# Decayed attention and two MoE layers on one core: where the attention stage does its side work

## The chip, the cores and the metric

The kernel runs on one core of a Trainium2 chip. The metric is device time in microseconds, from one execution of the whole program. The kernel before takes 567.04 us (median of three runs, 565.8 to 567.11).

## The reference

The input of the first MoE layer is the output of a linear attention with decay: 2 batches, 8 heads, 768 tokens, heads 64 wide. Per head there is one decay `lam`, and the reference goes over the tokens in blocks:

```python
for b in range(nb):
    intra = einsum('bhic,bhjc->bhij', qb, kb) * Dmask      # lam ** (i - j) for i >= j
    intra = einsum('bhij,bhjd->bhid', intra, vb)
    inter = einsum('bhid,bhde->bhie', qb * lam_pow, kv_state)
    out[:, :, sl] = intra + inter
    kv_state = lam_block * kv_state + einsum('bhsd,bhse->bhde', kb * rev_pow, vb)
```

Two MoE layers follow on 1536 tokens (512 features, 2048 hidden): `h = x @ w_in; g = h * clip(h + 3, 0, 6) / 6; y = g @ w_out`, and then `h = relu(y @ w_in2); out = (h * h) @ w_out2`.

## The kernel before

**Attention.** The 1536 tokens are cut into 12 chunks of 128 (`NC`), even chunks from batch 0, odd ones from batch 1; each batch has its own running state. A chunk goes through these steps, in the program's names:

- `load_chunk` (line 258): four transfers of 256 KB, kT, q, k and v, on the SP queue (only q of chunk 0 on ScalarE's queue). Five chunk buffers rotate.
- `scores` (350): TensorE multiplies keys and queries, 16 matmuls (L357), into a pair of PSUM banks; VectorE multiplies them by the decay mask into A (L368, two instructions).
- `prepare` (326): GpSimd multiplies the queries by the decay powers `lpow`, giving qs (L330); ScalarE multiplies the keys by their decay to the chunk's end, giving kd, in eight instructions of 128x64, one for each head (L342).
- `old_state` (378): TensorE multiplies qs by the state of two chunks ago, the same batch's last one (L389), into a bank px, of which there are two (`px_room`).
- `new_state` (396): TensorE multiplies kd and v (L407). ScalarE scales the old state by the chunk's decay into kvs, four instructions of 128x64 (L421), and VectorE adds the two in one instruction of 128x256 (L426; for the first chunk of a batch it only copies, L414).
- `values` (430): TensorE multiplies A and v into px (L440). ScalarE copies px to xf (L451, the first eight chunks only) and rounds it to xh (L453); VectorE writes the residual xl = px - xh (L456). With that the bank px is free again.

The decay masks and powers are made at the start by scans on VectorE (L308, L318). `warming` (295) runs matmuls of a zeroed tile that nothing reads.

**MoE.** TensorE multiplies in pairs of rounded and residual parts: `hidden` (L669), `quad` (L700, on sums of weights and of tokens in place of eight products) and `project` (L755). Weights come packed and are decoded by `decode` (501): two ScalarE instructions (L516, L520), three on VectorE (L525, L531, L535), the rounded part on ScalarE (L538), and a sum and the residual on VectorE (L539, L542). Three buffers for `w_in` tiles are there during the attention; the others open when its last chunk is through (`lend`, 481). `token_sums` (583) forms four sums and differences of 128x1024 of the tokens for the quads, once per layer, on VectorE (L596), and splits them (L616, L612, L614). `weight_sums` (551) does the same for weights on GpSimd (L563, L576).

**The order of the work.** The program first collects all operations in a list (`plan.op`), each with an engine, a cost from `COST`, what it needs and which buffers it takes and gives back. `Plan.run` (94) then lays them out in time: TensorE keeps the order of the list, and on the other engines the operation that can start first is taken next, by its due time where several can. GpSimd and those VectorE operations whose cost name begins with d are kept apart in time (`port`). The kernel issues instructions in the order that comes out, so costs and list order set the order of every queue. The chip then runs each queue in order, with waits on semaphores.

Of the kernel before, what the change touches and what calls it, by code (L numbers as in the profile page):

```python
# [9 lines left out]
F32 = mybir.dt.float32  # L10
# [4 lines left out]
AF = mybir.ActivationFunctionType  # L15
ALU = mybir.AluOpType
PSUM = bass.MemoryType.PSUM

P = 128
BLOCKS = 3  # L20
GROUP = 4
WARM = (8, 6)

COST = {
    "psc": 1.10, "inter": 1.02, "pst": 0.61, "av": 0.88, "unit": 2.72, "high": 1.81, "low": 0.91, "part": 1.36,
    "v512": (0.60, 0.69), "v256": (0.335, 0.42),
    "d512": (0.60, 0.69), "d512s": (0.36, 0.44), "d256": (0.335, 0.42), "d1024": (1.13, 1.21), "dsums": (1.35, 1.44),
    "s64x4": (0.50, 0.60), "s64x8": (1.00, 1.10),
    "s512": (0.53, 0.63), "s512r": (0.57, 0.67), "s512b": (0.59, 0.69), "s512p": (0.48, 0.59), "s1024": (0.96, 1.06),
    "p512": (1.30, 1.40), "p512b": (1.06, 1.16), "p256": (0.70, 0.80), "p1024": (2.40, 2.50), "psums": (3.30, 3.40),  # L30
    "load": (1.30, 3.60), "chunk": (0.66, 2.30),
# [24 lines left out]
class Plan:  # L56
# [111 lines left out]
def decay_attention_moe_moe(  # L168
# [47 lines left out]
    plan = Plan()  # L216
    op = plan.op

    def tile_of(shape, dt, tag, name=None):
        return sb.tile(shape, dt, tag=tag, name=name or tag)  # L220
# [12 lines left out]
        (py_room if slot < 3 else ph_room).free.append((slot, t))  # L233


    idle = tile_of([P, 512], F32, "lpow", "idle")
    nc.vector.memset(idle, 0.0)
    lams = tile_of([P, H + NP], F32, "lams")
    lam_h, lam_p = lams[:, :H], lams[:, H:]
# [15 lines left out]
    part = lambda c, n: chunk_t[chunk_hold[c].slot][:, ("kT", "k", "v", "q").index(n), :]  # L255
    loaded = {}

    def load_chunk(c):
        hold = chunk_hold[c]
        for n, src in (("kT", kT), ("q", qT), ("k", k), ("v", v)):  # L260

            def do(n=n, src=src):
                (nc.scalar if c == 0 and n == "q" else nc.sync).dma_start(out=part(c, n), in_=src[chunk_of[c]])

            loaded[c, n] = op("SP", "chunk", do, take=[hold], due=2.6 * c - 10)


    A_t = [tile_of([P, NP, 2, P], F32, f"A{i}") for i in range(2)]
    qs_t = tile_of([P, 2, NP, P], F32, "qs")
    kd_t = tile_of([P, 2, H, D], F32, "kd")  # L270
    lpow_t, kvs_t = {}, {}
    A_room, qs_room, kd_room = Room(0, 1), Room(0, 1), Room(0, 1)

    xh = [tile_of([P, KD, N], F32R, f"xh{j}") for j in range(BLOCKS)]
# [17 lines left out]
    s7_t = []  # L292


    def warming(widths):
        x = idle.bitcast(BF16)
        for n in widths:
            nc.tensor.matmul(banks[0][:, :n], x[:, :P], x[:, :n], start=True, stop=True)  # L298

    px_of, sums_in, s_hold = {}, {}, {}  # L300
    scans = []

    def attention():
        A_op, av_op, kv_op, qs_op, kd_op, int_op, kvs_op = {}, {}, {}, {}, {}, {}, {}
        A_hold, qs_hold, kd_hold, px_hold = {}, {}, {}, {}

        def scan_decay(h):
# [7 lines left out]
        def scan_power(a):  # L315
            if not a:
                lpow_t[0] = tile_of([P, NP, P], F32, "lpow")
            nc.vector.tensor_tensor_scan(  # L318
                lpow_t[0][:, a, :], lam_p[:, a : a + 1].to_broadcast([P, P]), zero.to_broadcast([P, P]), 1.0,
                op0=ALU.mult, op1=ALU.add,  # L320
            )

        for c in range(NC):
            load_chunk(c)

        def prepare(c):
            if c > 1:

                def do():
                    nc.gpsimd.tensor_tensor(  # L330
                        qs_t[:, qs_hold[c].slot].rearrange("p a i -> p (a i)"), part(c, "q"),
                        lpow_t[0].rearrange("p a i -> p (a i)"), op=ALU.mult,
                    )

                qs_hold[c] = Hold(qs_room)
                chunk_hold[c].left += 1
                qs_op[c] = op("POOL", "p512", do, [loaded[c, "q"], *scans], take=[qs_hold[c]], give=[chunk_hold[c]])
            if c < NC - 2:

                def do():  # L340
                    for h in range(H):
                        nc.scalar.activation(  # L342
                            kd_t[:, kd_hold[c].slot, h, :], part(c, "k")[:, h * D : (h + 1) * D], AF.Copy,
                            scale=decay[:, h // 2, h % 2, P - 1 : P],
                        )

                kd_hold[c] = Hold(kd_room)
                kd_op[c] = op("ACT", "s64x8", do, [loaded[c, "k"], *decays], take=[kd_hold[c]])

        def scores(c):  # L350

            def do():
                ps = [b.rearrange("p (a i) -> p a i", i=P) for b in pairs[hold.slot]]
                for a in range(NP):
                    i = slice(a * P, (a + 1) * P)
                    for t, r in enumerate(halves):
                        nc.tensor.matmul(  # L357
                            ps[t][:, a, :], part(c, "kT")[r, i], part(c, "q")[r, i], start=True, stop=True
                        )

            hold = Hold(pair_room, 2)
            hold.pass_on = pass_pair if c >= NC - 2 else None
            o = op("PE", "psc", do, [loaded[c, "kT"], loaded[c, "q"]], take=[hold])
            if not c:
                op("PE", 1.3, lambda: warming([512] * WARM[1]), [o])

            def mask(t):
                nc.vector.tensor_tensor(  # L368
                    A_t[A_hold[c].slot][:, :, t, :], pairs[hold.slot][t].rearrange("p (a i) -> p a i", i=P),
                    decay[:, :, t, :], op=ALU.mult,  # L370
                )

            A_hold[c] = Hold(A_room)
            A_op[c] = [
                op("DVE", "v512", lambda t=t: mask(t), [o, *decays], take=[A_hold[c]], give=[hold]) for t in range(2)
            ]
# [19 lines left out]
        def new_state(c):  # L396
            if c >= NC - 2:
                return
            first = c < 2
            kv_old, kv_new = kv[c % 2][(c // 2 + 1) % 2], kv[c % 2][c // 2 % 2]  # L400
            hold = Hold(pst_room)
            hold.pass_on = pass_bank if NC - 4 <= c else None
            ps = lambda: banks[hold.slot][:, : NP * D].rearrange("p (a d) -> p a d", d=D)

            def do():
                for h in range(H):
                    nc.tensor.matmul(  # L407
                        ps()[halves[h % 2], h // 2, :], kd_t[:, kd_hold[c].slot, h, :], part(c, "v")[:, h * D : (h + 1) * D],
                        start=True, stop=True,
                    )  # L410

            pst = op("PE", "pst", do, [kd_op[c], loaded[c, "v"]], take=[hold], give=[kd_hold[c]])
            if first:
                kv_op[c] = op("DVE", "v256", lambda: nc.vector.tensor_copy(kv_new, ps()), [pst], give=[hold])  # L414
            else:
                s = Hold(ts_room)

                def scale():
                    kvs_t[c] = tile_of([P, KD, HALF], F32, "Ts", f"kvs{c}")[:, :, :D]
                    for a in range(NP):  # L420
                        nc.scalar.activation(kvs_t[c][:, a, :], kv_old[:, a, :], AF.Copy, scale=lpow_t[0][:, a, P - 1 : P])  # L421

                kvs_op[c] = op("ACT", "s64x4", scale, [kv_op[c - 2], *scans], take=[s])
                readers = [int_op.get(c - 2), kvs_op.get(c - 2)]
                kv_op[c] = op(
                    "DVE", "v256", lambda: nc.vector.tensor_tensor(kv_new, ps(), kvs_t.pop(c), op=ALU.add),  # L426
                    [pst, kvs_op[c], *readers], give=[hold, s],
                )

        def values(c):  # L430
# [27 lines left out]
            )  # L458
            x_ops[0, j] += [hi, lo]

        prepare(0)
        scores(0)
        for a in range(NP):
            scans.append(op("DVE", "v256", lambda a=a: scan_power(a)))
        prepare(1)
        new_state(0)
        old_state(0)
        values(0)
        scores(1)
        for c in range(1, NC):  # L470
            if c + 1 < NC:
                scores(c + 1)
                prepare(c + 1)
            old_state(c)
            new_state(c)
            values(c)
        return av_op

    lent = {}
# [103 lines left out]
    def token_sums(layer, old):  # L583
# [8 lines left out]
        def add(n, tag, a, b, sign, needs, take, give=()):  # L592

            def do():
                stage[n] = tile_of([P, KH, N], F32, tag, f"s{n}")
                nc.vector.tensor_tensor(stage[n], a(), b(), op=sign)  # L596

            return op("DVE", "d1024", do, needs, take=take, give=give)

        def split(n, o, give, wait=()):  # L600

# [201 lines left out]
    nc.gpsimd.memset(zero, 0.0)  # L803
    nc.gpsimd.memset(three, 3.0)
    warming([512] * WARM[0])
    plan.clock.update(PE=4.3, DVE=3.0, ACT=1.5, POOL=3.5, SP=1.0)
    attention()


# [126 lines left out]
```

## Time and profile before

| | |
|---|---|
| median of three runs | 567.04 us |
| the profiled execution | 565.54 us |
| its span, first to last instruction | 563.7 us |
| TensorE busy | 554.6 us, 98% |
| VectorE busy | 398.7 us, 71% |
| ScalarE busy | 348.4 us, 62% |
| GpSimd busy | 89.2 us, 16% |
| mean granted TensorE clock | 0.996 |

All times of the trace count from the start of the span. In the rows, PE is TensorE and PEld its weight loads, DVE is VectorE, ACT is ScalarE, POOL is GpSimd and SP is the sync engine, from which most transfers start; L342 is line 342 of the kernel. The granted clock is a share of 2.4 GHz: 1.00 is that level, 0.50 is 1.2 GHz. Busy shares are averages over the two stages, which differ much, so the rows below are taken stage by stage.

### The profile page before, as it was taken

What the parts mean: (1) busy time and instruction counts of PE and PEld (TensorE: products, weight loads), DVE (VectorE), ACT (ScalarE), POOL (GpSimd) and SP (SyncE); (2) the same over time, 40 slices, a digit from 0 to 9 for tenths busy, and PEclk for the clock granted to TensorE, in tenths of its full rate; (3) what the DMA queues carried; (4) which work ended last, traced back from release to release, by engine and by line L of the source; (5) the groups of instructions that cost most, each with busy time, mean ns of one, the idle gap of its engine ahead of it and who ended that gap; (6) DMA issues with size and microseconds to landing.
All of it is one profiled execution on the core that took longest, in us unless ns stands there. A gap on an engine that the chain in (4) does not pass through costs nothing.

```text
span 563.7 us, 7855 instructions
## 1 busy us (share of the span) xinstructions
PE 554.6 (98%) x2950; PEld 458.0 (81%) x2950; DVE 398.7 (71%) x647; ACT 348.4 (62%) x657; POOL 89.2 (16%) x78
## 2 busy tenths in 40 slices
PE   8988999999999999999999999999999999999997
PEld 6877888888888888888888888888888888888885
DVE  6759999858894698659999885138792589446222
ACT  6996885658552676148655996368752896168120
POOL 2230004330312103210000003210320121210000
PEclk9998999999999999999999999999999999999999
DMA  8982323302230032202330331102230033000112
GB/s 315 407 326 77 112 76 112 112 1 76 74 130 21 11 122 93 74 0 76 106 119 0 100 124 39 37 1 82 98 120 1 25 126 112 1 0 1 74 58 93
DMA packets 18038, 49.80 MB, mean 88 GB/s; under 512 B 2128, under 2 KB 2128, under 8 KB 18000
## 3 DMA queue, kind: packets, MB, share of 16 engines
q1 hardware_dynamic: 17856, 49.04, 24.9%
q8 instruction: 23, 0.38, 0.3%
q10 hardware_dynamic: 144, 0.26, 0.1%
q14 instruction: 15, 0.12, 0.1%
HBM read 46.14 MB, written 3.15 MB: 87 GB/s over the span
## 4 chain that ended last, share of the span: by engine, by line
PE 94%; ACT 5%; DVE 0%; issue 0%
PE b L755 46%; PE b L669 23%; PE b L700 20%; ACT kd L342 2%; PE b L357 1%; PE b L440 1%; PE b L389 1%; PE b L298 1%; ACT kvs L421 1%; PE b L407 1%; ACT xh L453 1%; ACT xf L451 0%; ACT da L516 0%; ACT dt L520 0%; DVE xl L456 0%
## 5 line engine op out<-in xcount | busy, mean ns | idle before, releaser
L779 DVE TENSOR_TENSOR acc<-acc,b 128x512 f32<-128x512 f32 x72 | 49.3, 686 | 62.1 <-PE b L755 61.9
L669 PE MATMUL b<-xh,wi 128*128 128x512 f32 x240 | 76.6, 389 | 0.0
L755 PE MATMUL b<-gC,wo 128*128 128x512 f32 x228 | 70.0, 389 | 0.0
L755 PE MATMUL b<-wo,gC 128*128 128x512 f32 x228 | 68.7, 389 | 0.0
L563 POOL TENSOR_TENSOR Tsum<-dt,dt 128x256 f32<-128x256 f32 x12 | 15.7, 1308 | 276.2 <-DVE dt L539 142.6
L669 PEld LDWEIGHTS b<-xh,wi 128*128 128x128 f32 x240 | 45.1, 188 | 9.5 <-issue 0.2
L650 ACT ACTIVATE gs<-b 128x512 f32<-128x512 f32 x48 | 28.1, 590 | 37.7 <-PE b L669 15.0
L535 DVE SCALAR_TENSOR_TENSOR da<-raw,da 128x512 int32<-128x512 int32 x64 | 50.3, 797 | 0.9
L644 ACT ACTIVATE gs<-b,three 128x512 f32<-128x512 f32 x48 | 32.6, 685 | 29.0 <-PE b L700 16.5
L755 PEld LDWEIGHTS b<-gC,wo 128*128 128x128 f32 x228 | 42.8, 188 | 8.9
L755 PEld LDWEIGHTS b<-wo,gC 128*128 128x128 f32 x228 | 42.8, 188 | 8.9
L516 ACT ACTIVATE da<-raw 128x512 f32<-128x512 f32 x64 | 42.1, 670 | 7.6 <-DVE dt L539 7.1
L669 PE MATMUL b<-xl,wi 128*128 128x512 f32 x120 | 46.7, 389 | 0.0
L576 POOL TENSOR_TENSOR Tl<-Tsum,Th 128x1024 fp32r<-128x1024 f32 x12 | 29.2, 2437 | 103.9 <-ACT Th L571 103.9
L539 DVE CUSTOM_DVE_ANT_0 dt<-da,dt 128x1024 uint16<-128x1024 uint16 x64 | 43.4, 689 | 1.4 <-ACT gs L651 0.2
L520 ACT ACTIVATE dt<-raw 128x512 int32<-128x512 uint32 x64 | 42.2, 668 | 3.0 <-DVE wi L542 1.7
L647 DVE SCALAR_TENSOR_TENSOR gs<-gs,b 128x512 f32<-128x512 f32 x48 | 32.7, 687 | 11.2 <-ACT gs L644 11.2
L654 DVE TENSOR_TENSOR gC<-gs,gC 128x512 fp32r<-128x512 f32 x38 | 27.3, 726 | 18.1 <-ACT gC L652 18.1
L755 PE MATMUL b<-g,wo 128*128 128x512 f32 x120 | 38.9, 389 | 0.0
L755 PE MATMUL b<-wo,g 128*128 128x512 f32 x120 | 37.6, 389 | 0.0
L755 PE MATMUL b<-gA,wo 128*128 128x512 f32 x120 | 37.6, 389 | 0.0
L755 PE MATMUL b<-wo,gA 128*128 128x512 f32 x108 | 36.2, 389 | 0.0
(131 smaller groups left out, 1214.8 us busy)
## 6 DMA issues: line engine op xcount, KB each, us to landing
raw<-in_w_in SPq DMA_DIRECT2D x32, 512.0 KB, 3.4
raw<-in_w_out SPq DMA_DIRECT2D x32, 512.0 KB, 3.3
out<-acc SPq DMA_DIRECT2D x12, 256.0 KB, 2.0
inC<-in_kT SPq DMA_DIRECT2D x6, 256.0 KB, 5.3
inC<-in_k SPq DMA_DIRECT2D x6, 256.0 KB, 5.1
inC<-in_v SPq DMA_DIRECT2D x6, 256.0 KB, 5.1
inS<-in_kT SPq DMA_DIRECT2D x6, 256.0 KB, 5.7
inS<-in_qT SPq DMA_DIRECT2D x6, 256.0 KB, 6.0
```

The lines of the kernel that those rows point to most:

```text
L516: "ACT", "s512r", lambda: nc.scalar.activation(abs_t[a.slot], r(1).bitcast(F32), AF.Abs, scale=2.0**16),
L520: "ACT", "s512r", lambda: nc.scalar.activation(up(), r(0).bitcast(U32), AF.Copy, scale=2.0**-29),
L535: lambda: nc.vector.scalar_tensor_tensor(u(), r(1), -(2**31), u(), op0=ALU.bitwise_and, op1=ALU.bitwise_or),
L539: add = op("DVE", "d512", lambda: nc.vector.tensor_tensor(up(), u(), up(), op=ALU.add), [join, low], give=[a])
L576: "POOL", "p1024", lambda: nc.gpsimd.tensor_tensor(at["l"], at["f"], at["h"].bitcast(F32), op=ALU.subtract),
L644: a = op("ACT", "s512b", lambda: nc.scalar.activation(s(), ps(), AF.Relu, bias=three), [done], take=[st])
L647: lambda: nc.vector.scalar_tensor_tensor(s(), s(), 6.0, ps(), op0=ALU.min, op1=ALU.mult), [a], give=bank,
L650: a = op("ACT", "s512p", lambda: nc.scalar.activation(s(), ps(), AF.Relu), [done], take=[st], give=bank)
L669: nc.tensor.matmul(ps(), u, x[:, a, :], start=a == 0 and i == 0, stop=a == KD - 1 and i == 2)
L700: nc.tensor.matmul(t, p0, p1, start=start and a == 0 and n == 0, stop=a == KH - 1 and n == 2, skip_group_check=True,)
L755: nc.tensor.matmul(ps(), u, y, start=f == fs[0] and i == 0, stop=f == fs[-1] and i == 2)
L779: "DVE", "v512", lambda: nc.vector.tensor_tensor(t(), t(), ps(), op=ALU.add), [low, old[e]], give=[bank],
```

## The change

It touches the attention stage and the place of the token sums:

- the old state is no longer scaled on ScalarE; VectorE computes old state x decay + new product in one instruction per pair of heads (four of 128x64), reading the new product from PSUM;
- of the decayed keys ScalarE makes four heads, and GpSimd the other four in one instruction of 128x256;
- kT and q of chunks 0 and 1 are loaded ahead of v and k of either; the scores of both come first on TensorE, and in later chunks the scores of the next chunk follow the old-state product and the new state, in place of standing ahead of them;
- the six warming matmuls behind the first scores become three and three, and the zeroed tile has another place;
- the token sums (L596) go to GpSimd;
- the planner's costs and its starting clock for SP follow.

```diff
-WARM = (8, 6)
+WARM = (8, 3)
-    "s64x4": (0.50, 0.60), "s64x8": (1.00, 1.10),
+    "s64x4": (1.00, 1.12), "v64x4": (0.52, 0.60), "p256b": (0.53, 0.62),
...
-    idle = tile_of([P, 512], F32, "lpow", "idle")
+    idle = tile_of([P, 2 * DM], F32, "Tl", "idle")[:, :512]
...
-        for c in range(NC):
-            load_chunk(c)
+        for n, (c, names) in enumerate(
+            [(0, "kT q"), (1, "kT q"), (0, "v k"), (1, "v k")] + [(c, "kT q k v") for c in range(2, NC)]
+        ):
+            for x in names.split():
+                load(c, x, 2.6 * max(n - 2, 0) - 10)
...
-                    for h in range(H):
+                    for h in range(H // 2):
                         nc.scalar.activation(
...
+                def others():
+                    nc.gpsimd.tensor_tensor(
+                        kd_t[:, kd_hold[c].slot, H // 2 :],
+                        part(c, "k").rearrange("p (h d) -> p h d", d=D)[:, H // 2 :],
+                        decay.rearrange("p a t i -> p (a t) i")[:, H // 2 :, P - 1 : P].to_broadcast([P, H // 2, D]),
+                        op=ALU.mult,
+                    )
...
-                def scale():
-                    kvs_t[c] = tile_of([P, KD, HALF], F32, "Ts", f"kvs{c}")[:, :, :D]
+                def state():
                     for a in range(NP):
-                        nc.scalar.activation(kvs_t[c][:, a, :], kv_old[:, a, :], AF.Copy, scale=lpow_t[0][:, a, P - 1 : P])
+                        nc.vector.scalar_tensor_tensor(
+                            kv_new[:, a, :], kv_old[:, a, :], lpow_t[0][:, a, P - 1 : P], ps()[:, a, :],
+                            op0=ALU.mult, op1=ALU.add,
+                        )
...
-                    "DVE", "v256", lambda: nc.vector.tensor_tensor(kv_new, ps(), kvs_t.pop(c), op=ALU.add),
-                    [pst, kvs_op[c], *readers], give=[hold, s],
+                    "DVE", "v64x4", state, [pst, kv_op[c - 2], int_op.get(c - 2), *scans], give=[hold],
...
-        prepare(0)
         scores(0)
+        scores(1)
         for a in range(NP):
-            scans.append(op("DVE", "v256", lambda a=a: scan_power(a)))
-        prepare(1)
-        new_state(0)
-        old_state(0)
-        values(0)
-        scores(1)
-        for c in range(1, NC):
-            if c + 1 < NC:
+            scans.append(op("DVE", "v256", lambda a=a: scan_power(a), [A_op[0][1]]))
+        for c in range(NC):
+            prepare(c)
+            old_state(c)
+            if c < 2:
+                op("PE", 0.65, lambda c=c: warming([512] * WARM[1], c), [warm_after[c]])
+            if c == 1:
+                scores(2)
+            if c > 1:
+                new_state(c)
+            if c > 1 and c + 1 < NC:
                 scores(c + 1)
-                prepare(c + 1)
-            old_state(c)
-            new_state(c)
             values(c)
+            if c < 2:
+                new_state(c)
...
-                nc.vector.tensor_tensor(stage[n], a(), b(), op=sign)
-
-            return op("DVE", "d1024", do, needs, take=take, give=give)
+                nc.gpsimd.tensor_tensor(stage[n], a(), b(), op=sign)
+
+            return op("POOL", "p1024", do, needs, take=take, give=give)
...
-    plan.clock.update(PE=4.3, DVE=3.0, ACT=1.5, POOL=3.5, SP=1.0)
+    plan.clock.update(PE=4.3, DVE=3.0, ACT=1.5, POOL=3.5, SP=2.0)
```

## Rows read from the trace of the kernel before

**Rows 1.** Windows table: stretch, length, each engine's busy us, clock, DMA share, GB/s

```profile
1.45:17.15 15.70, 15.70 (x191) 11.23 (x191) 11.34 (x25) 11.65 (x41) 2.97 (x3) 1.00 1.00 361
17.15:53.47 36.32, 32.39 (x531) 27.92 (x529) 26.09 (x47) 30.90 (x102) 9.92 (x8) 0.95 0.73 280
53.47:560.00 506.53, 506.51 (x2234) 418.90 (x2232) 360.13 (x574) 305.85 (x516) 75.59 (x60) 1.00 0.20 67
...
44.21:48.28 4.07, 4.07 (x48) 3.57 (x48) 3.97 (x8) 2.05 (x7) 1.28 (x1) 0.58 0.23 93
...
10.00:37.50 27.50, 25.78 (x455) 22.54 (x456) 17.75 (x32) 27.50 (x93) 10.32 (x8) 1.00 1.05 406
...
53.54:80.80 27.26, 27.26 (x121) 22.57 (x121) 26.98 (x46) 23.69 (x39) 0.00 (x0) 1.00 0.31 98
```

**Rows 2.** Chain that ended last, in order of time: start, us, what; one chunk

```profile
33.78 1.92 ACT kd L342 x8
35.70 0.96 ACT kvs L421 x4
36.66 0.47 ACT xf L451
37.12 0.48 ACT xh L453
```

**Rows 3.** Waits: engine, line, waited for: us in total, times, longest

```profile
DVE xl L456 <- ACT xh L453: 5.0, 7, 1.3
...
PE b L389 <- DVE xl L456: 3.7, 4, 2.1
```

**Rows 4.** Timeline of TensorE: start, us, line, operation, count, idle before and releaser

```profile
17.15 1.16 PE L357 MATMUL b<-inS 64*128 64x128 f32 x16
18.24 1.09 PE L389 MATMUL b<-qs,states 64*64 64x128 f32 x16
...
20.75 1.16 PE L357 MATMUL b<-inC 64*128 64x128 f32 x16
...
32.44 1.16 PE L357 MATMUL b<-inS 64*128 64x128 f32 x16 [0.16 <-DMA inS<-in_qT]
...
44.21 1.97 PE L389 MATMUL b<-qs,states 64*64 64x128 f32 x16 [2.06 <-DVE xl L456]
...
48.28 1.16 PE L357 MATMUL b<-inC 64*128 64x128 f32 x16
```

**Rows 5.** Timeline of the first microseconds, ScalarE and TensorE

```profile
5.49 1.28 ACT L342 ACT_TABLE_LOAD   x1 [5.49 <-DMA inC<-in_k]
6.78 3.92 ACT L342 ACTIVATE kd<-inC,decay 128x64 f32<-128x64 f32 x16
...
6.86 1.47 PE L298 MATMUL b<-idle 128*128 128x512 bf16 x6
```

**Rows 6.** Groups by line and shape, to 53.54 us: count, busy us, mean ns, idle before

```profile
L368 DVE TENSOR_TENSOR A<-b,decay 128x512 f32<-128x512 f32 x24 | 15.8, 683 | 3.8 <-PE b L357 3.8
...
L330 POOL TENSOR_TENSOR qs<-inC,lpow 128x512 f32<-128x512 f32 x4 | 5.1, 1276 | 13.1 <-PE b L389 7.9 <-PE b L440 2.8 <-DMA inC<-in_qT 2.5
...
L426 DVE TENSOR_TENSOR states<-b,kvs 128x256 f32<-128x256 f32 x8 | 3.4, 419 | 3.6 <-ACT kvs L421 3.6
...
L318 DVE TENSOR_TENSOR_SCAN lpow<-lams,zero 128x128 f32<-128x128 f32 x4 | 1.4, 405 | 0.2 <-PE b L298 0.2
```

**Rows 7.** Timeline about 101 us, GpSimd and VectorE

```profile
101.40 2.57 POOL L576 TENSOR_TENSOR Tl<-Tsum,Th 128x1024 fp32r<-128x1024 f32 x1 [4.48 <-ACT Th L571]
...
101.62 2.89 DVE L542 TENSOR_TENSOR wi<-dt,wi 128x512 fp32r<-128x512 f32 x1
```

**Rows 8.** Timeline from 53 to 81 us: a token sum, a weight tile, its user

```profile
53.75 1.22 DVE L596 TENSOR_TENSOR s<-xf 128x1024 f32<-128x1024 f32 x1
...
75.28 0.70 DVE L542 TENSOR_TENSOR wo<-dt,wo 128x512 fp32r<-128x512 f32 x1
...
80.80 0.39 PE L755 MATMUL b<-g,wo 128*128 128x512 f32 x1
```

More of the change, by code (lines that the diff above doesn't have):

```diff
@@ L256, in decay_attention_moe_moe, with load, do @@
     loaded = {}
[L258 to L265, printed above, removed]
+    def load(c, n, due):
+        src = {"kT": kT, "q": qT, "k": k, "v": v}[n]
+        def do():
+            (nc.scalar if c == 0 and n == "q" else nc.sync).dma_start(out=part(c, n), in_=src[chunk_of[c]])
+        loaded[c, n] = op("SP", "chunk", do, take=[chunk_hold[c]], due=due)
     A_t = [tile_of([P, NP, 2, P], F32, f"A{i}") for i in range(2)]
@@ L270, in decay_attention_moe_moe @@
     kd_t = tile_of([P, 2, H, D], F32, "kd")
-    lpow_t, kvs_t = {}, {}
+    lpow_t = {}
     A_room, qs_room, kd_room = Room(0, 1), Room(0, 1), Room(0, 1)
@@ L292, in decay_attention_moe_moe, with warming @@
     s7_t = []
-    def warming(widths):
+    def warming(widths, bank=0):
         x = idle.bitcast(BF16)
         for n in widths:
-            nc.tensor.matmul(banks[0][:, :n], x[:, :P], x[:, :n], start=True, stop=True)
+            nc.tensor.matmul(banks[bank][:, :n], x[:, :P], x[:, :n], start=True, stop=True)
     px_of, sums_in, s_hold = {}, {}, {}
@@ L303, in attention @@
     def attention():
-        A_op, av_op, kv_op, qs_op, kd_op, int_op, kvs_op = {}, {}, {}, {}, {}, {}, {}
+        A_op, av_op, kv_op, qs_op, kd_op, int_op = {}, {}, {}, {}, {}, {}
         A_hold, qs_hold, kd_hold, px_hold = {}, {}, {}, {}
@@ L338, in prepare, with some @@
             if c < NC - 2:
-                def do():
-                    for h in range(H):
+                def some():
+                    for h in range(H // 2):
                         nc.scalar.activation(
@@ L345, in do @@
                         )
-                kd_hold[c] = Hold(kd_room)
-                kd_op[c] = op("ACT", "s64x8", do, [loaded[c, "k"], *decays], take=[kd_hold[c]])
+                def others():
[5 more added lines that the diff above has]
+                    )
+                kd_hold[c] = Hold(kd_room)
+                kd_op[c] = [
+                    op(e, cost, f, [loaded[c, "k"], *decays], take=[kd_hold[c]])
+                    for e, cost, f in (("POOL", "p256b", others), ("ACT", "s64x4", some))
+                ]
+        warm_after = {}
         def scores(c):
@@ L362, in scores @@
             hold.pass_on = pass_pair if c >= NC - 2 else None
-            o = op("PE", "psc", do, [loaded[c, "kT"], loaded[c, "q"]], take=[hold])
-            if not c:
-                op("PE", 1.3, lambda: warming([512] * WARM[1]), [o])
+            o = warm_after[c] = op("PE", "psc", do, [loaded[c, "kT"], loaded[c, "q"]], take=[hold])
             def mask(t):
@@ L410, in do @@
                     )
-            pst = op("PE", "pst", do, [kd_op[c], loaded[c, "v"]], take=[hold], give=[kd_hold[c]])
+            pst = op("PE", "pst", do, [*kd_op[c], loaded[c, "v"]], take=[hold], give=[kd_hold[c]])
             if first:
@@ L415, in new_state @@
             else:
-                s = Hold(ts_room)
-                def scale():
-                    kvs_t[c] = tile_of([P, KD, HALF], F32, "Ts", f"kvs{c}")[:, :, :D]
+                def state():
                     for a in range(NP):
-                        nc.scalar.activation(kvs_t[c][:, a, :], kv_old[:, a, :], AF.Copy, scale=lpow_t[0][:, a, P - 1 : P])
-                kvs_op[c] = op("ACT", "s64x4", scale, [kv_op[c - 2], *scans], take=[s])
-                readers = [int_op.get(c - 2), kvs_op.get(c - 2)]
+                        nc.vector.scalar_tensor_tensor(
+                            kv_new[:, a, :], kv_old[:, a, :], lpow_t[0][:, a, P - 1 : P], ps()[:, a, :],
+                            op0=ALU.mult, op1=ALU.add,
+                        )
                 kv_op[c] = op(
-                    "DVE", "v256", lambda: nc.vector.tensor_tensor(kv_new, ps(), kvs_t.pop(c), op=ALU.add),
-                    [pst, kvs_op[c], *readers], give=[hold, s],
+                    "DVE", "v64x4", state, [pst, kv_op[c - 2], int_op.get(c - 2), *scans], give=[hold],
                 )
```

## The prediction

> **What bounds the kernel now.** I read the windows table first. From 53.47 us to 560 us TensorE is busy for 506.51 of 506.53 us at full clock: both MoE layers are one unbroken block of matmuls, and an edit there can only lose time [rows 1]. The attention stage before it falls into two parts. From 1.45 to 17.15 TensorE is busy for 15.70 of 15.70 us. From 17.15 to 53.47 it is busy for 32.39 of 36.32, at a mean clock of 0.95 [rows 1]. So whatever can be won lies between 17.15 and 53.47.
>
> The chain of waits names the cause. Nearly all of it between 17 and 43 us runs over ScalarE. In one chunk the eight decayed keys take 1.92 us, the scaling of the old state 0.96, the full copy of the output 0.47 and its rounding 0.48, together 3.83 us [rows 2]. The TensorE timeline gives the pace to compare: from the scores of chunk 4 at 17.15 to those of chunk 5 at 20.75 is 3.60 us without a gap [rows 4]. ScalarE needs 0.23 us more per chunk than TensorE, before it does any weight decoding, and falls behind. The waits show where this comes out. The product with the old state (L389) waits 3.7 us in four places for the residual xl (L456), which frees its PSUM bank; xl itself had waited for the rounding on ScalarE [rows 3]. The longest of these waits is 2.06 us, ahead of 44.21 [rows 4]. After it the granted clock is 0.58 on average, and 4.07 us go on L389, L407 and L440 of one chunk [rows 1], which make 2.51 at full clock (3.60 less the 1.09 from 17.15 to 18.24 for the scores) [rows 4]. That is 1.56 us.
>
> What the stage would take without these losses: 17.15, plus seven periods of 3.60, plus the end from 48.28 to 53.47 (the scores of chunk 11 and four products, 5.19 us) makes 47.54 [rows 1, 4]. It takes 53.47, so 5.93 us are lost: 3.9 in idle TensorE, 1.56 at the lower clock, 0.5 in small gaps. 5.9 us is also the most that the change can win here.
>
> **The change part by part.**
>
> *ScalarE.* Half of the decayed keys leave (0.96 us a chunk) and all of the state scaling (0.96). What stays is 0.96 + 0.47 + 0.48 = 1.91 us of each 3.60, so the decoding of the first three weight tiles (L516, L520, L538) finds room and xl is no longer late for want of ScalarE. This takes the cause of the 3.9 us away, and with the 2.06 us wait the low clock.
>
> *VectorE.* The state was one add of 128x256 at 0.419 us and becomes four instructions on 128x64. Their operation is not in the trace. By columns: (0.683 - 0.419)/256 = 1.03 ns a column between the adds of 256 and 512 (L426, L368), so 64 columns take 0.419 - 192 x 0.00103 = 0.22 us; four make 0.88. The bounds are 0.07 us (64 columns and nothing else) and 0.405 us (the scan of 128 columns, L318) [rows 6]. I take 0.22, nearest to the add that is replaced. VectorE is busy for 26.09 us from 17.15 on [rows 1]; seven states add 7 x (0.88 - 0.42) = 3.2, which makes 29.3 in the 30.4 us that TensorE would need. That is tight. But the decoding of the second and third weight tile is in it, and they are not needed when the MoE stage starts, so they can slip. I count no loss, and keep it as a rival.
>
> *GpSimd.* It gets the other half of the keys, 128x256: half of the 1.28 us of the 128x512 product (L330) is 0.64; at worst as much as the whole, 1.28 [rows 6]. With L330 that is 1.9 to 2.6 us of 3.60, and the keys come with the same chunk as the queries, well ahead of their matmuls. Hidden on either count. Should this cover go (GpSimd a whole chunk late), L407 would wait in every chunk.
>
> *The head.* The chunk loads are reordered: k of chunk 0 goes from the third to the sixth transfer. It landed at 5.49, where ScalarE's table load starts behind it [rows 5]. Three transfers of 262 KB at 361 GB/s [rows 1] are 2.2 us, so 7.7. Table load 1.28 and four activations of 0.245 (16 take 3.92) [rows 5] end at 9.9. TensorE gets there sooner: scores of chunk 0 to 6.9, of chunk 1 1.1 more, three warming matmuls 0.7 (half of the six), values of chunk 0 some 1.0, together 9.7 at most [rows 4, 5]. So L407 of chunk 0 waits at least 0.2 us, and behind it in TensorE's order wait the other warming matmuls, the scores of chunk 2 and all later work. Bounds: 0, and 1.1 if the transfers arrive at half the speed of that window's mean at first. I take 0.6. Nothing is won in the head, since TensorE is full there already; warming matmuls are six before and after. The power scans (L318) wait for the mask of chunk 0, behind which they ran before anyway.
>
> *TensorE's order.* The old-state product now stands directly behind the values of the chunk before, ahead of the next scores. It needs the bank of two chunks ago, so the copy, the rounding and xl have 3.60 us instead of 4.69 (one set of scores more). Undisturbed they take 0.47 + 0.48 + 0.68 (xl is as wide as the masks of L368) and some 0.3 of hand-over, 1.9 us [rows 2, 6]; 1.7 are left for what stands ahead of them on the two engines. Both at once (half the keys on ScalarE, two masks on VectorE, 0.96 + 1.36) is 0.6 too much. I take one such meeting, 0.6; at each of seven chunks it would be 4.
>
> *Transfers.* The scores of chunk 8 waited 0.16 us for their queries at 32.44 [rows 4]; the queues move 406 GB/s then, with a share of 1.05 [rows 1]. In the new order L389 of chunk 7 starts at 17.75 + 4 x 3.60 = 32.15 (17.15, and 0.6 of the head), and these scores behind it and L407, 1.5 later, at 33.7: 1.2 us later than their data. Cost nothing, with 1.2 us of cover.
>
> *Token sums on GpSimd.* The eight sums of 128x1024 took 1.22 us each on VectorE [rows 8] and take about 2.57, as the subtraction L576 does [rows 7]. GpSimd has idle time enough, and no matmul needs the sums for some 50 us. Yet the rows show a price: L576 started at 101.40, and the VectorE subtraction L542, which started at 101.62 and otherwise takes 0.69, took 2.89 and ended just behind it [rows 7]. So a sum can hold a VectorE instruction for 2.2 us. The Trainium skill (SBUF — State Buffer, Who interferes with whom) gives this as a rule: a GpSimd instruction that reads SBUF and a VectorE instruction with two SBUF inputs exclude each other for a whole instruction, and the one that starts first wins. The trace agrees (2.89 us). By that rule the sums are a rival, below; in the sum I count nothing, since VectorE is also rid of 8 x 1.22 us.
>
> **Sum.** 47.54 + 0.6 (head) + 0.6 (bank) + 0.5 (small gaps, as before) = 49.2 against 53.47: 4.2 us less. The MoE block follows unchanged. The profiled execution took 565.54 (span 563.7 and 1.8 around it), so 561.3. It lies 1.5 us under the median of the runs, 567.04; from the median the forecast is 562.8.
>
> **The rivals.**
>
> *VectorE takes ScalarE's place, and it gets slower.* Place: from 17.15 to the MoE stage. Busy time there is 26.09 + 7 x (4d - 0.42) for d us per state instruction; with it stay the 5.0 us for which it waited on xh [rows 3]. At d = 0.405 that is 34.5 + 5.0 = 39.5 us, end at 17.75 + 39.5 = 57.2, and 3.8 us more than before: 570.8. It decides from d = 0.26 on (36.3 - 0.6 - 5.0 - 26.1 = 4.6 for seven states). For it: VectorE at 97% by my own count. Against: the columns give 0.22, most of the waiting on xh goes with ScalarE's load, and decoding can slip.
>
> *The transfers eat it.* If the loads of weights move two places ahead of chunk 8 (524 KB at 406 GB/s are 1.3 us each), its scores wait 2.6 - 1.2 = 1.4 us; with the head at its bound of 1.1, the gain is 4.2 - 1.4 - 0.5 = 2.3: 564.7. For it: queues full from 10 to 37.5 us. Against: the due times of the weights are the same.
>
> *The port takes it back.* From 53.54 to 80.80 VectorE is busy for 26.98 of 27.26 us [rows 1]. Four sums that each hold it for 2.2 are 8.8; one of its own (1.22) is gone before the last weight tile that the first output projection needs, which starts at 75.28 and is done at 75.98, 4.8 us ahead of TensorE at 80.80 [rows 8]. So TensorE waits 7.6 - 4.8 = 2.8 us there; a wait of 2.06 cost 1.5 in clock before, so 4.3 in all, and the gain is gone: 567.1. For it: the row of 2.89. Against: many VectorE instructions read PSUM, and by 80.8 up to four of its sums are gone.
>
> **How the numbers follow.** The forecast, with a gain of 3 to 5.9, gets 0.60: its own range is 561.1 to 564.0. Transfers (or other waits that leave 1.7 to 3 us) 0.20, port 0.11, VectorE 0.09. A measurement tells 0.3% (1.7 us) from no change; by that faster is 0.60 + 0.20 = 0.80, the same 0.11, slower 0.09. The range for 8 in 10 starts at 560.2, since the runs before spread by 0.6 around their middle and may centre on the profiled one, and ends at 565.8, beyond the second rival.
>
> **What would show it.** Right: MoE's first matmul (L669) near 49 us; ScalarE no longer in the chain from 17 on; no TensorE wait above 1 us there, and a clock of 1.00; states at about 0.2 us per instruction; L407 of chunk 0 waiting for ScalarE by about half a microsecond. Wrong: TensorE idle behind xl again, with VectorE at 97% (first rival); the scores waiting for queries (second); or an L755 that waits for a weight tile around 75 us (third).

## The result: slower, and the profile after

The changed kernel takes 572.87 us (median of five runs, 571.9 to 573.23) against 567.11 beside it: a ratio of 1.010, 95% interval 1.0082 to 1.0117. The forecast was 562.8, faster. Its profiled execution took 572.11 us, with a span of 570.3 against 563.7 of before, so there are 6.6 us to place.

The windows table of after (columns as in [rows 1]) shows the attention:

```profile
1.45:17.15 15.70, 15.70 (x185) 11.31 (x187) 11.07 (x27) 7.25 (x21) 6.22 (x7) 1.00 1.00 362
17.15:40.00 22.85, 22.48 (x384) 19.25 (x382) 21.30 (x46) 16.78 (x44) 12.51 (x13) 1.00 1.04 396
40.00:50.00 10.00, 6.66 (x110) 5.55 (x106) 9.91 (x16) 0.58 (x1) 6.35 (x4) 1.00 0.14 56
50.00:60.00 10.00, 8.76 (x64) 7.19 (x65) 8.04 (x13) 5.06 (x9) 2.35 (x1) 0.83 0.15 55
```

Up to 40 us TensorE is full but for 0.37 us. Then it idles for 3.3 of 10 us, ScalarE has almost nothing to do, VectorE is full and GpSimd, at 6.35 us, busier than anywhere else. The waits of TensorE (as [rows 3]) name the two places of the whole run where it idles:

```profile
PE b L449 <- DVE A L379: 2.8, 2, 2.6
PE b L400 <- DVE xl L465: 2.2, 3, 1.5
PE b L766 <- ACT gC L663: 1.4, 1, 1.4
PE b L766 <- DVE acc L790: 0.5, 1, 0.5
```

The first two stand in the attention, all but 0.4 us of them in its last three chunks; the others are at the boundary of the two MoE layers. (xl is the residual that frees a PSUM bank, A the masked scores, acc the accumulator of an output, gC a buffer of hidden values.) In TensorE's timeline (as [rows 4]):

```profile
17.57 1.09 PE L400 MATMUL b<-qs,states 64*64 64x128 f32 x16
...
21.33 1.09 PE L400 MATMUL b<-qs,states 64*64 64x128 f32 x16
...
42.27 1.09 PE L400 MATMUL b<-qs,states 64*64 64x128 f32 x16 [1.54 <-DVE xl L465]
...
50.79 0.43 PE L449 MATMUL b<-A,inC 128*64 128x128 f32 x2 [2.59 <-DVE A L379]
51.39 1.97 PE L449 MATMUL b<-A,inC 128*64 128x128 f32 x14 [0.17 <-DVE A L379]
...
56.37 0.50 PE L680 MATMUL b<-xh,wi 128*128 128x512 f32 x1
```

The MoE stage starts at 56.37, where before had 53.47 and the forecast 49.2. And a full chunk takes 3.76 us (17.57 to 21.33), not the 3.60 of [rows 4]. What holds the masks at 50 us is seen by laying two timelines side by side, first GpSimd's, then VectorE's:

```profile
43.49 1.29 POOL L331 TENSOR_TENSOR qs<-inC,lpow 128x512 f32<-128x512 f32 x1 [4.09 <-PE b L400]
44.74 2.36 POOL L607 TENSOR_TENSOR s<-xf 128x1024 f32<-128x1024 f32 x1
47.17 2.41 POOL L607 TENSOR_TENSOR s<-s,xf 128x1024 f32<-128x1024 f32 x1
49.66 2.69 POOL L607 TENSOR_TENSOR s<-xf,s 128x1024 f32<-128x1024 f32 x1
```

```profile
44.93 2.45 DVE L542 TENSOR_SCALAR da<-da 128x512 int32<-128x512 int32 x1
47.41 2.72 DVE L546 SCALAR_TENSOR_TENSOR da<-raw,da 128x512 int32<-128x512 int32 x1
50.05 1.28 DVE L379 TENSOR_TENSOR A<-b,decay 128x512 f32<-128x512 f32 x2
51.25 1.65 DVE L550 CUSTOM_DVE_ANT_0 dt<-da,dt 128x1024 uint16<-128x1024 uint16 x1
```

Three token sums run one after the other, right behind the last chunk's queries in GpSimd's queue. What they read, the full copies xf, had been complete since 39.15, so it was that queue that set their start. Beside each stands one decoding instruction of VectorE (0.42 to 0.69 us otherwise) that started later and ends just after it. The masks of chunk 10 (its scores ran from 43.90 on) are behind the first two of these in VectorE's queue and start at 50.05. The masks themselves, which read one operand from PSUM, take their usual 1.28 us beside the third sum: they are not held, they are late. The Trainium skill (SBUF — State Buffer, Who interferes with whom) has the rule that only instructions which need the shared port pair exclude each other; held L542 and L546 (2.45 and 2.72 us), unheld L379 (1.28) agree with it.

The rest of the 6.6 us lies behind the attention: from the first matmul of the MoE stage to the end after takes 513.9 us and before 510.2. About 1.9 of these 3.7 are the two waits at the boundary, where the second layer's sums hold VectorE in the same way (GpSimd, VectorE, TensorE):

```profile
298.28 2.70 POOL L607 TENSOR_TENSOR s<-s,acc 128x1024 f32<-128x1024 f32 x1 [11.36 <-DVE acc L790]
```

```profile
298.84 2.70 DVE L553 TENSOR_TENSOR wikd<-dt,wikd 128x512 fp32r<-128x512 f32 x1
```

```profile
302.79 0.73 PE L766 MATMUL b<-gdecay,wo 128*128 128x512 f32 x2 [0.53 <-DVE acc L790]
...
341.19 0.74 PE L766 MATMUL b<-wo,gC 128*128 128x512 f32 x2 [1.39 <-ACT gC L663]
```

And 1.4 us come without any wait. The groups of L711 (columns: count, busy us, mean ns), the products of a layer that work on sums, show slower matmuls where Tl, the residual part of the summed weights, takes part or stands next in the order; before, all of these took 389 ns:

```profile
L711 PE MATMUL b<-Ssum,Th 128*128 128x512 f32 x96 | 29.9, 392 | 0.0
L711 PE MATMUL b<-xh,Tl 128*128 128x512 f32 x48 | 19.1, 397 | 0.0
L711 PE MATMUL b<-Ssum,Tl 128*128 128x512 f32 x48 | 19.1, 397 | 0.0
L711 PE MATMUL b<-xl,Th 128*128 128x512 f32 x48 | 19.0, 396 | 0.0
```

48 x (8 + 8 + 7) + 96 x 3 ns = 1.4 us. What changed is the place of tiles: the idle tile is now allocated first under the name Tl, so Tl went from byte 216,320 of each partition to byte 1,152. Nearly all other tiles moved too, most of them by 2,048 bytes.

So the account: attention +2.9, boundary about +2.3, Tl +1.4; sum 6.6. Of the 2.3 at the boundary 1.9 are the two waits. The 0.4 left over stay open: the clock doesn't explain them, as the granted clock is 1.00 around both waits.

### The profile page after: what moved, and what is told of

It is laid out like the page before. It is cut to its first block, busy times and chain, and to the rows that moved or that the text cites. A ratio compares the mean times of both kernels' runs of the same rounds, so it can differ in the third digit from the quotient of the medians.

```text
span 570.3 us, 7823 instructions
## 1 busy us (share of the span) xinstructions
PE 558.2 (98%) x2950; PEld 459.3 (81%) x2950; DVE 408.8 (72%) x663; ACT 331.8 (58%) x585; POOL 117.2 (21%) x96
## 4 chain that ended last, share of the span: by engine, by line
PE 75%; DVE 15%; ACT 5%; DMA 2%; issue 1%; SPq 1%; DVEq 0%; ACTq 0%
PE b L766 40%; PE b L711 19%; PE b L680 16%; DMA inS<-in_k 2%; DVE da L546 2%; DVE xl L803 1%; DVE A L379 1%; DVE dt L550 1%; DVE acc L790 1%; DVE da L536 1%; DVE da L542 1%; DVE states L430 1%; ACT gs L662 1%; DVE Ssum L625 1%; DVE gs L658 1%
## 5 line engine op out<-in xcount | busy, mean ns | idle before, releaser
L546 DVE SCALAR_TENSOR_TENSOR da<-raw,da 128x512 int32<-128x512 int32 x64 | 50.7, 804 | 1.0
L550 DVE CUSTOM_DVE_ANT_0 dt<-da,dt 128x1024 uint16<-128x1024 uint16 x64 | 45.2, 717 | 1.1 <-ACT gs L662 0.2
L766 PE MATMUL b<-gA,wo 128*128 128x512 f32 x108 | 36.2, 389 | 0.0
L542 DVE TENSOR_SCALAR da<-da 128x512 int32<-128x512 int32 x64 | 34.7, 548 | 1.4
```

The costliest lines, as they stand in the source:

```text
L542: "DVE", "d512s", lambda: nc.vector.tensor_scalar(u(), u(), 3, None, op0=ALU.logical_shift_left), [clamp]
L546: lambda: nc.vector.scalar_tensor_tensor(u(), r(1), -(2**31), u(), op0=ALU.bitwise_and, op1=ALU.bitwise_or),
L550: add = op("DVE", "d512", lambda: nc.vector.tensor_tensor(up(), u(), up(), op=ALU.add), [join, low], give=[a])
L766: nc.tensor.matmul(ps(), u, y, start=f == fs[0] and i == 0, stop=f == fs[-1] and i == 2)
```

## The experiments

All were timed in five rounds beside the kernel before (its medians 566.39 to 566.98). Each edit is against the kernel named.

**The sums back on VectorE; the idle tile elsewhere; both.** Against the changed kernel:

```diff
-                nc.gpsimd.tensor_tensor(stage[n], a(), b(), op=sign)
+                nc.vector.tensor_tensor(stage[n], a(), b(), op=sign)
-            return op("POOL", "p1024", do, needs, take=take, give=give)
+            return op("DVE", "d1024", do, needs, take=take, give=give)
```

```diff
-    idle = tile_of([P, 2 * DM], F32, "Tl", "idle")[:, :512]
+    idle = tile_of([P, 512], F32, "gs2", "idle")
```

> The changed kernel with the token sums back on VectorE, all else as changed. Theory (a token sum on GpSimd holds VectorE's decoding instructions, which stand ahead of the masks and residuals in VectorE's queue): the long waits of TensorE between 42 and 56 us and near 302 and 340 us go; the MoE stage starts near 51.3 us in place of 56.4; some 566.4 us at the median of before (567.1), since 1.4 us of slower matmuls with Tl stay. Rival (VectorE is simply full, the state instructions are too many for it): it now has 4.9 us more of its own work per layer, the MoE stage starts at 55 or later, and the time stays at 570 or above.

> The changed kernel with the zeroed tile of the warming matmuls in the space of a gs tile, so that Tl lies again where it lay in the kernel before; all else as changed. Theory (the matmuls next to Tl take 397 in place of 389 ns because Tl has moved): they are back at 389 ns and the time is 1.4 us shorter than that of the changed kernel, 571.4. Rival (something else in the quads, the clock or the order, makes them slower): 396 to 397 ns stay, and so does the time, 572.9.

> Both of these undone: sums on VectorE, zeroed tile in the space of a gs tile; the attention part of the change stays. Theory: the sum of the two, 565.0 us, 2 us faster than before. Rival of a full VectorE: 569 or above.

Sums back: 564.35 us, ratio 0.9956 (0.9944 to 0.9969), so 8.5 us less than the changed kernel and 2 us less than the theory had; both waits at the boundary are gone. VectorE runs the same instructions in the same order, unheld, and the masks start 3.9 us sooner; below them is the start of MoE in TensorE's timeline:

```profile
45.12 0.42 DVE L542 TENSOR_SCALAR da<-da 128x512 int32<-128x512 int32 x1
45.58 0.69 DVE L546 SCALAR_TENSOR_TENSOR da<-raw,da 128x512 int32<-128x512 int32 x1
46.19 1.28 DVE L379 TENSOR_TENSOR A<-b,decay 128x512 f32<-128x512 f32 x2
```

```profile
51.54 0.50 PE L680 MATMUL b<-xh,wi 128*128 128x512 f32 x1
```

Idle moved: 571.96, 0.9 less, which the spread of these two kernels' runs doesn't settle (571.81 to 573.43 against 571.9 to 573.23). But the Tl matmuls are at 389 ns again:

```profile
L711 PE MATMUL b<-xh,Tl 128*128 128x512 f32 x48 | 18.7, 389 | 0.0
```

Both: 563.32, ratio 0.9934 (0.9921 to 0.9948). Moving the idle tile is worth 1.0 us here, with runs that don't overlap (562.93 to 563.76 against 564.21 to 564.91 with the sums alone put back). The sums are the loss, the moved tiles a second, small one, and the two add. This edit puts every moved tile back, so it shows that the places matter, not that it is Tl's own place. Without both the change does gain, 3.7 us, but its attention ends at 51.68 and not at 49.2. Three things are left in it: the period of 3.76 us, a wait of 0.88 for the queries of chunk 1 in the first microseconds, and one late bank, here in the timelines of GpSimd, VectorE and TensorE:

```profile
38.48 1.26 POOL L331 TENSOR_TENSOR qs<-inC,lpow 128x512 f32<-128x512 f32 x1 [0.59 <-PE b L400]
```

```profile
38.53 1.76 DVE L550 CUSTOM_DVE_ANT_0 dt<-da,dt 128x1024 uint16<-128x1024 uint16 x1
...
41.77 0.69 DVE L465 TENSOR_TENSOR xl<-b,xh 128x512 fp32r<-128x512 f32 x1
```

```profile
7.19 1.16 PE L371 MATMUL b<-inC 64*128 64x128 f32 x16 [0.88 <-DMA inC<-in_qT]
...
42.60 1.09 PE L400 MATMUL b<-qs,states 64*64 64x128 f32 x16 [1.54 <-DVE xl L465]
```

**The sums alone.** Before, with only its sums on GpSimd (the first diff, turned round).

> The kernel before with the token sums on GpSimd, and nothing else of the change. Theory: the sums fall again on the decoding beside the last chunks and on the layer boundary; 2 to 3 us lost at the end of the attention and 2.2 near 300 to 340 us: 571 to 572. Rival (the sums are harmless, the attention part is at fault): 567.1.

586.33 us, ratio 1.0341 (1.0326 to 1.0356): worse than in the changed kernel, and 14 us above the theory's 571 to 572, so only its direction held. VectorE's timeline has the same two held instructions, and here it is xl that stands behind them:

```profile
50.16 2.45 DVE L531 TENSOR_SCALAR da<-da 128x512 int32<-128x512 int32 x1
52.64 2.71 DVE L535 SCALAR_TENSOR_TENSOR da<-raw,da 128x512 int32<-128x512 int32 x1
55.27 0.68 DVE L456 TENSOR_TENSOR xl<-b,xh 128x512 fp32r<-128x512 f32 x1
```

```profile
PE b L755 <- ACT acc L770: 9.7, 1, 9.7
PE b L389 <- DVE xl L456: 9.6, 5, 5.5
```

The wait of 9.7 is another price. The accumulator acc lies in the space of xf, so its first copies (L770, ScalarE) must follow the sums that read xf, and the plan had put them behind much decoding.

**The order of scores and old state.** Against the kernel with both undone:

```diff
+            if c > 1 and c + 1 < NC:
+                scores(c + 1)
             old_state(c)
...
-            if c > 1 and c + 1 < NC:
-                scores(c + 1)
             values(c)
```

> The kernel with both undone (sums on VectorE, zeroed tile in a gs tile), and the scores of the next chunk again ahead of the old-state product and the new state. Theory (between chunks 3 and 9 the new order itself costs TensorE: a period is 3.75 us in place of 3.60, since matmuls on 64 rows and on 128 rows change places four times in a chunk in place of twice; and it shortens the time that xl has to free its bank): the period is 3.60 again, the MoE stage starts 1.2 us sooner, and up to 1.5 more if the wait for xl at 42.6 goes too; 560.6 to 562.1 us. Rival (the order of the same matmuls is free): 563.3.

561.11 us, ratio 0.9911 (0.9897 to 0.9924), 2.2 less. From 27 us on TensorE's timeline is dense at a period of 3.60 again, and the wait of 1.54 for xl is gone. One wait is left (TensorE, then VectorE):

```profile
26.77 1.09 PE L400 MATMUL b<-qs,states 64*64 64x128 f32 x16 [0.82 <-POOL kd L349]
...
30.37 1.09 PE L400 MATMUL b<-qs,states 64*64 64x128 f32 x16
...
33.98 1.09 PE L400 MATMUL b<-qs,states 64*64 64x128 f32 x16
...
48.88 0.50 PE L680 MATMUL b<-xh,wi 128*128 128x512 f32 x1
```

```profile
25.94 0.68 DVE L465 TENSOR_TENSOR xl<-b,xh 128x512 fp32r<-128x512 f32 x1
```

The row puts this wait down to the keys, but the old state doesn't read them. It is xl again: it ends at 26.62, 0.15 before the start, as it did ahead of the wait of 1.54. MoE starts 2.8 us sooner (51.68 to 48.88). Not all of that is the order's: 0.88 of it is the transfer wait, which this execution didn't have, and the 0.82 was lost again.

In this order (the old one) matmuls of 64 rows (scores, old state) stand together and those of 128 rows (new state, values) too, with two changes of kind per chunk. The change's order (old state, new state, scores, values) has four, and takes 0.15 us more without a wait in between. That the changes of kind cost it fits the rows; another cause that comes with this order was not tried.

**Keys by ScalarE alone.** All eight keys of a chunk on ScalarE again, with their measured cost in the plan, first in the change's order and then in the old one, both with the sums and the idle tile undone:

```diff
-                    for h in range(H // 2):
+                    for h in range(H):
...
-                    for e, cost, f in (("POOL", "p256b", others), ("ACT", "s64x4", some))
+                    for e, cost, f in (("ACT", "s64x8", some),)
```

> The kernel with both undone, and all eight decayed keys again on ScalarE, with its true cost in the planner; GpSimd has only qs. Theory (the wait of 1.5 us for xl at 42.6 comes of decoding instructions on VectorE that GpSimd's two instructions per chunk hold up, 1.3 to 1.8 us each in place of 0.7): they are back near 0.7, the wait goes, ScalarE has 2.9 of 3.75 us per chunk and still keeps up; 561.8. Rival 1 (VectorE is full without any hold): the wait stays, 563.3. Rival 2 (ScalarE binds again): 565 or above.

> Both of the first two together: the kernel with both undone, old place of the scores, all keys on ScalarE. Only the state on VectorE, the order of loads and the head are left of the change. Theory: 560.0 to 561.5, if ScalarE at 2.9 of 3.60 us per chunk keeps up. Rival (half of the keys on GpSimd are needed): 563 or above.

564.07 (ratio 0.9965, 0.9952 to 0.9979) and 563.39 (0.9952, 0.9939 to 0.9966), both above what their theories had. In the first the wait at 42 us went, as the theory had it, but another of 2.35 for xl came at 24.55; in the second TensorE waits 2.0 us for xl ahead of 25.12. ScalarE, busy without a gap before, rounds late there (xh is done at 22.53 and 22.75), and VectorE has other work ahead of xl for 1.2 and 1.5 us more (xl starts at 23.72 and 24.29). So the half of the keys on GpSimd is worth 2.3 us (563.39 to 561.11), in spite of the VectorE instructions it holds.

**State scaling by ScalarE.** The version of 561.11, with kvs on ScalarE (four instructions) and one add on VectorE, as before:

```diff
-                        nc.vector.scalar_tensor_tensor(
-                            kv_new[:, a, :], kv_old[:, a, :], lpow_t[0][:, a, P - 1 : P], ps()[:, a, :],
+                        nc.scalar.activation(kvs_t[c][:, a, :], kv_old[:, a, :], AF.Copy, scale=lpow_t[0][:, a, P - 1 : P])
...
+                    "DVE", "v256", lambda: nc.vector.tensor_tensor(kv_new, ps(), kvs_t.pop(c), op=ALU.add),
```

> The same version, with the scaling of the state again on ScalarE in a tile of its own and one add on VectorE; half of the keys stay on GpSimd. ScalarE then has 1.92 + 0.95 = 2.87 us a chunk instead of 1.91, still below the 3.60 of TensorE. Theory (ScalarE's load alone made it late): 562 to 564, as much as giving ScalarE the other half of the keys back cost (2.3 us), with waits for xl of 1 to 2 us. Rival: the scaled state shares its space with the first token sum, as in the kernel before, and waits for it: a TensorE wait of several us for the state near 45 us and 566 or more.

560.23 us, ratio 0.9891 (0.9876 to 0.9906): both theories missed. It is the fastest version of all, MoE starts at 48.45 and TensorE's whole list of waits for data behind the first microseconds is two transfers:

```profile
PE b L371 <- DMA inC<-in_qT: 0.4, 1, 0.4
PE b L371 <- DMA inS<-in_qT: 0.3, 1, 0.3
```

With half of the keys gone ScalarE does its 2.87 us per chunk in time, and moving the state as well gains nothing. Whether it costs the 0.9 us between the two medians is not settled, as their intervals overlap.

**Only the planner's costs.** The kernel before has 0.50 and 1.00 us in its plan for instructions of ScalarE that take 0.96 and 1.92 [rows 2]; the change corrects that too. Alone:

```diff
-    "s64x4": (0.50, 0.60), "s64x8": (1.00, 1.10),
+    "s64x4": (0.96, 1.08), "s64x8": (1.92, 2.04),
```

> The kernel before with nothing but true costs for the ScalarE instructions of 128x64 in the planner (0.96 for four and 1.92 us for eight, in place of 0.50 and 1.00). Theory (ScalarE has 3.83 us of work per 3.60, which no order mends): 566.5 to 567.5. Rival (what was won came from a planner that knows the costs, not from moving the work): 563 to 565.

572.63 us, ratio 1.0112 (1.0098 to 1.0126): slower, where both theories had no loss. The chunks from 23 to 44 us ran without a wait, but then the old state waited, in TensorE's and ScalarE's timelines:

```profile
55.28 1.97 PE L389 MATMUL b<-qs,states 64*64 64x128 f32 x16 [10.10 <-DVE states L426]
```

```profile
53.16 1.06 ACT L421 ACTIVATE kvs<-states,lpow 128x64 f32<-128x64 f32 x4 [1.30 <-DVE Ssum L612]
```

The plan now let the first token sum take the tile Ts at 40.25 us, and the scaled state shares that tile. One true number in a plan moved a large wait into the kernel; so the change's costs can't be judged apart from its order.

**The second layer's sums alone** on GpSimd, and **the first layer's alone**, in the version of 561.11. For the first layer the first sum was to start behind the attention's last values: once in the planner's list, once held by data.

```diff
+        o1 = add(1, ..., [*got[1], *([] if layer else [last_av[0]])], [h1])
```

```diff
+            def gate():
+                t = tile_of([P, KH, N], F32, "Ts", "gate")
+                nc.vector.tensor_copy(t[:, 0, :1], xl[2][:, 0, N - 1 :].bitcast(F32))
```

> The same version, with the second layer's sums alone on GpSimd. Theory: the changed kernel's loss of 2.2 us between the layers comes from these four sums, which hold decoding and accumulation on VectorE: the time is 563 to 564 (561.1 and about 2.2), with TensorE waits of 0.5 and 1.4 us at the layers' boundary. Rival: that loss was a consequence of the shifted plan, not of the sums: the time is 561 to 562, as without them.

> The version with the old order of scores and products, the idle tile out of the way and the sums on VectorE took 561.1. Here the sums of the first layer alone go to GpSimd, and the first of them is held until the attention's last values; the second layer's stay on VectorE. Theory: the sums cost in the attention because they start beside its last chunks, where VectorE's decoding is held and the masks wait behind it. Held back, the attention ends as without them: MoE starts near 48.9 us, no mask is late, and the time is 561 to 563 (what is left is a late weight tile in the first layer, if any). Rival: GpSimd's sums cost wherever decoding stands beside them, since each holds a VectorE instruction for 2.4 us: then the loss only moves into the first layer, a wait of TensorE for a weight tile near 75 us, and the time is 564 or more.

> The run before with the first layer's sums on GpSimd moved them only in the planner's order: on the chip the first still started at 43.17 us, as its data was ready and nothing stood ahead of it in GpSimd's queue. Here it is held by data: one column of the last chunk's xl is first written into the tile that the first sum takes. All else as in the version of 561.1 us. Theory (place beside the attention's last chunks): no TensorE wait above 1 us before the MoE stage, which starts at 48.9 to 49.2 us instead of 52.84, with a clock of 1.00; from there the sums hold VectorE's decoding, which has 20 us of lead, so the first weight tiles still come in time; the accumulator copies may stay behind the sums, as before, and then TensorE waits near 90 us, which the waits will show on its own line. Rival (the attention's end gets late whatever the sums' place): MoE starts at 51 us or later.

Second layer: 564.01 us, ratio 0.9958 (0.9946 to 0.9971), 2.7 us above the version without by the two ratios (2.9 by the medians), as the theory had it, or a little more, with the same two waits (0.57 and 1.40).

First layer, by the list: 577.97 us, ratio 1.0202 (1.0187 to 1.0217). The experiment did not hold the sums. GpSimd's timeline:

```profile
43.17 2.36 POOL L607 TENSOR_TENSOR s<-xf 128x1024 f32<-128x1024 f32 x1
45.60 2.67 POOL L607 TENSOR_TENSOR s<-s,xf 128x1024 f32<-128x1024 f32 x1
```

The list only sets the order in each queue; behind the last queries nothing else stood in GpSimd's, and the sums ran at once. MoE starts at 52.84, and an acc copy held TensorE for 10.4 us at 98.87.

First layer, by data: 578.9 us, ratio 1.0218 (1.0204 to 1.0232). One sum of the four still ran at 43.55, the three others from 81.81 on. TensorE's waits (its lines from L639 on stand 8 further down):

```profile
PE b L774 <- ACT acc L789: 15.2, 1, 15.2
PE b L400 <- DVE xl L465: 0.7, 1, 0.7
```

The attention ends at 49.66, where the theory had 48.9 to 49.2 and the rival 51 or more: with three sums out of it, 3.2 of the 4.0 us that the sums cost there (52.84 less 48.88) are gone. Of the 0.8 that remain, 0.6 were there before any sum ran: the scores of chunk 4 start at 17.96 here and at 17.36 in the version of 561.11. So the place decides for the attention. But late sums make the acc copies late, and that wait is larger than what was saved.

## Why the prediction was wrong, step by step

- **The token sums: the step that failed.** It said "I count nothing". They cost 8.5 us by the medians (572.87 to 564.35) and 7.5 by the spans (570.3 to 562.8): 4.8 of these in the attention (56.37 to 51.54), 2.7 behind it. (Ahead of any sum, at the old state of chunk 3, the two profiled executions stand at 17.57 and 18.25, so the spans hide some 0.7 of the cost.) The row of 2.89 us [rows 7] was the mechanism, and the third rival priced it, at 4.3, but at the wrong place: it put the sums at 53.75, where before has them [rows 8]. There the queue of VectorE held them back. GpSimd's queue is nearly empty, so they start right behind the last queries, beside the last chunks, where decoding stands ahead of masks in VectorE's order. The argument that VectorE is rid of 8 x 1.22 us missed that each held instruction makes all behind it late. And the planner keeps GpSimd's and VectorE's port users apart only in its own clock; the chip keeps the order in each queue and not those times (the sum that the list put behind the last values started at 43.17).
- **TensorE's order.** I priced one late bank at 0.6. It was one wait of 1.54, and a period of 3.76 instead of 3.60 that I had taken over from the old order, some 1.1 more over seven chunks. The old order has a late bank of 0.82 of its own; it saves 2.2 us by the medians.
- **The idle tile.** Not in the sum at all: a change of a tile's name moved other tiles and cost 1.4 us by the rows, 1.0 in the medians of the pair that is clear of the spread.
- **ScalarE.** Right: it is out of the way until 40 us, and the clock there is 1.00. That both of its jobs have to leave is not so: with half of the keys gone and the state scaling kept, 560.23, no wait for it is among TensorE's.
- **VectorE.** Right: four state instructions take 0.85 us (forecast 0.88), in the row below, and the first rival's point of 0.26 us each is not reached. VectorE was put at 29.3 us of work from 17.15 on; the version of 561.11 has 29.20 there.

```profile
40.67 0.85 DVE L430 SCALAR_TENSOR_TENSOR states<-states,lpow,b 128x64 f32<-128x64 f32 x4
```

- **GpSimd's keys.** 0.61 to 0.67 us unheld (forecast 0.64), and hidden after the head (the wait that a row puts down to them, at 26.77, is xl's), but they and the queries hold decoding as well (1.76 instead of 0.69 above). I had seen the exclusion in [rows 7] and applied it to the sums alone.
- **The head and the transfers.** Of the 0.6 about 0.4 was lost: the work that before has done at 17.15 is done at 17.57. TensorE counts as full there all the same, since a stretched group counts as busy: the new state of chunk 0, which was to wait for its keys, takes 0.97 us, that of chunk 1 0.64. The rest of the 0.4 are several terms of about 0.1, and in before the new state of chunk 0 was stretched too. No wait for a transfer shows in the changed kernel's execution, but in that of both undone the queries of chunk 1 came 0.88 late; the forecast's bound of 1.1 for late transfers was put on the keys of chunk 0.
- **The sum.** The attention without losses was put at 47.54 and the stage's end at 49.2; with the three terms undone it ends at 48.88, and the kernel at 561.11, its profiled execution at 561.55 against 561.3 of the sum. So near a match is in part luck: it comes with another order of TensorE than the one that was forecast. Of its 1.34 us above 47.54, 0.82 are one late bank (forecast 0.6) and 0.2 the head (0.6); the rest are small gaps. What stands between, about 10.8 us from 561.3 to 572.11, are in the attention 4.7 of sums (56.37 to 51.68) and 2.8 of the order and the late queries of chunk 1 (51.68 to 48.88), less the 0.3 by which 48.88 is under 49.2, then 2.3 at the boundary and 1.4 of Tl.

## What to carry to other kernels

An operation moved to an idle engine starts when its data is there and the little ahead of it is done, not when it used to: look for what runs beside that moment, and what is queued behind it. When two engines exclude each other, price the held instruction by everything behind it in its in-order queue. And list what an edit moves that it doesn't name: a buffer that is allocated first changes the addresses of others.

## What the runs showed of the hardware

- A GpSimd 128x1024 instruction (2.4 us) made VectorE instructions on SBUF alone last as long as itself, even with one input (0.42 to 2.45 us), and left the masks, which read PSUM, alone (1.28).
- The same matmuls took 389 ns with Tl at byte 216,320 and 397 at byte 1,152 of each partition, in two pairs of kernels; most other tiles moved by 2,048 bytes between them. Which place matters, and why, is open.
- Four products of one chunk took 3.60 us in one order and 3.76 in another, each without a wait of TensorE for another engine.
